# Cluster masks for the last seven pairs of heads: from TensorE products to VectorE writes ahead of the scores

## The chip, the core and the metric

One core of a Trainium2 chip runs the kernel. TensorE multiplies matrices into PSUM, VectorE and ScalarE work on PSUM and SBUF, GpSimd (POOL in the profile) on SBUF only, and DMA queues move data. The engines run side by side and wait for one another by semaphores; each takes its own instructions in program order. The metric is the time of one execution on the device in microseconds, the median of several runs.

## The reference

Attention in which a query sees only the keys of its own cluster, and behind it a feed-forward network on the result.

```python
B, H, S, D = 4, 8, 768, 64           # batch, heads, positions, head size; 16 clusters per head
q_assign = argmax(q_n @ c_n.T)       # q_n, k_n, c_n: rows scaled to length one
k_assign = argmax(k_n @ c_n.T)
mask   = q_assign[..., :, None] == k_assign[..., None, :]
scores = where(mask, q @ k.T / sqrt(D), -1e9)
attn   = softmax(scores)
x      = (attn @ v)                  # -> (3072 tokens, 512)
h = x @ w_in                         # 512 -> 2048
g = h * clip(h + 3, 0, 6) / 6
out = g @ w_out                      # 2048 -> 512
```

## The kernel before

Heads go in 16 pairs (4 pairs are a batch). A pair has 12 items: two halves of 384 queries times six chunks of 128 keys. An item is a 128 x 768 block of scores (keys x queries, both heads of the pair), in one of two buffers `ps`. Items are worked in steps of two; r is the number of the step's first item within its pair (0, 2, ... 10).

A masked score is made by two products that add up in PSUM: a product of one-hot cluster vectors in bf16 (`xm`; the keys' side is 1 outside the key's cluster and scaled by -2^60), and the product of keys and queries in f32 (`xf`). Where the clusters differ, -2^60 is added, and the exponential is zero.

```python
def route_turn(g, part):                     # turns the one-hots of pair g: xm
    ...
    po = scratch([P, NCH, P], "po", BF16)
    for i in range(NCH):
        nc.tensor.transpose(out=po[:, i], in_=one_hot[:, part * NCH + i], identity=ident_q)
    dst = xm[:, part * NCH : (part + 1) * NCH]
    nc.scalar.activation(out=dst, in_=po, func=ACT.Copy, scale=-FAR if part else 1.0)

def scores_part(n, x, first, last):
    g, hf, j = where(n)
    for t in range(2):                       # the two heads
        r = slice(t * D, (t + 1) * D)
        nc.tensor.matmul(st["ps", n][:, t, 0:HALF], lhsT=x[r, NCH + j],
                         rhs=x[r, hf * NHC : (hf + 1) * NHC], start=first, stop=last)
# scores(n): scores_part(n, xm, True, False), then scores_part(n, xf, False, True)

def exponentials(n):                         # ScalarE, ps -> ex; frees the buffer ps
    ...
def attn_v(n):                               # TensorE: pv += v * ex (two heads); behind item 5 of
    ...                                      # a half, ScalarE copies pv to num
def divide(n):                               # behind the last item of a half
    ...
    pd = scratch([P, 512], "pd")
    for t in range(2):
        nc.tensor.matmul(pd[t * D : (t + 1) * D], lhsT=ones, rhs=acc[:, t], start=True, stop=True)
    rcp = nump.tile([P, HALF], F32, name="rcp")
    nc.vector.reciprocal(out=rcp, in_=pd)
    nc.vector.tensor_tensor(out=num, in0=num, in1=rcp, op=ALU.mult)
    ...
```

`scratch` in the second half of the kernel takes its tile from a PSUM pool of one buffer (`psum_t`); `pd`, the transposes `pqk` of keys and queries, the cluster scores `pcs`, their transposes `pr` and `po` all use it. The network's products use another pool of two buffers (`psum_m`).

From pair 8 on, two kinds of steps alternate. At r = 2, 6, 10 ("fill steps") there are two scores products, two exponentials, then four or five items of the feed-forward network, with the preparation of the next pair spread among them. At r = 0, 4, 8 ("value steps") there are two scores products, two exponentials and the value products of four items, and at r = 4 and r = 8 a division.

```python
def four_by_four(n, r, steps):
    for i in steps:
        scores(i)
    if r % 4 == 2:                           # fill step: the items follow in the main loop
        for i in steps:
            exponentials(i)
        unmasked.extend(steps)
        check_all()
        ...
        return
    for i in steps[: 1 if r == 8 else 2]:
        exponentials(i)
    check_all()
    for i in unmasked:
        masks(i)                             # nothing: no pair is masked by VectorE here
        key_sums(i)                          # GpSimd: acc += ex
    unmasked.clear()
    if r == 4 or n >= total:
        ...
            later.append(divide(m))
    for i in range(st["valued"], min(n, total)):
        attn_v(i)
        if i % per_pair == NCH - 1:          # this is at r = 8
            later.append(divide(i))
    st["valued"] = min(n, total)
    for i in steps[1 if r == 8 else 2 :]:
        exponentials(i)
    for i in steps:
        masks(i)
        key_sums(i)

# main loop, pair 8 on
prep = ...      # of the next pair: r = 2: three turns (pqk); r = 6: cluster scores, route; r = 10: one-hots turned
if prep and r == (6 if fours else 4):
    prep.pop(0)()
...
for i in range(max(len(prep), want)):        # want: four or five
    if i < want:
        fill.pop(0)()
    if i < len(prep):
        prep[i]()
```

The feed-forward items of a block of 256 tokens are 8 "up" and 7 "down" items. An up item (`halved`) makes two PSUM tiles, uX and uY, from the pool of two, and VectorE adds them up:

```python
X = psum_m.tile(..., name="uX", tag="m")
part(X[:, 0], ...); part(X[:, 1], ...); part(X[:, 2], ...)         # TensorE
nc.vector.tensor_copy(out=sx[:, 1], in_=X[:, 1])
add(sx[:, 0], X[:, 0], sx[:, 1]); add(sx[:, 2], X[:, 2], sx[:, 0]) # VectorE
Y = psum_m.tile(..., name="uY", tag="m")
part(Y[:, 0], ...); ... part(Y[:, 3], ...)                         # TensorE
add(sx[:, 3], Y[:, 0], sx[:, 0]); add(g[:, 3], Y[:, 0], sx[:, 2])
add(g[:, 0:3], Y[:, 1:4], sx[:, 1:4])                              # VectorE
lift(sx, g)                                                        # ScalarE
finish()                       # clip (VectorE) and sums (GpSimd) of the up item before
```

A down item multiplies `g_sb` with the second weights into tiles X and Y of the same pool; VectorE has little to do there.

Of the kernel before, what the change touches and what calls it, by code (L numbers as in the profile page):

```python
# [8 lines left out]
F32 = mybir.dt.float32  # L9
# [8 lines left out]
C = 16  # L18
# [98 lines left out]
def fast_path(ctx, tc, ok, q, k, v, centroids, moe_w_in, moe_w_out, out):  # L117
# [48 lines left out]
    counts = const.tile([P, 2, NPAIR], F32, name="counts")  # L166
    w_low = const.tile([P, 1], F32, name="w_low")

    MASKED = NPAIR
    st = {}  # L170
    later = []
    numbers = []
# [87 lines left out]
    cen = startp.tile([P, D], F32, name="cen")  # L260
    parity = const.tile([P, 2], F32, name="parity")

    number = const.tile([P, C], BF16, name="number")

    def constants():
        make_identity(nc, ident)
        for t in range(2):
            nc.vector.tensor_reduce(
                out=parity[:, t : t + 1],
                in_=ident.rearrange("p (h t c) -> p t h c", t=2, c=C)[:, t], axis=AX.XY, op=ALU.max,  # L270
            )
        nc.gpsimd.memset(half_c, 0.5)
        nc.gpsimd.memset(low_c, 1.0 / BOUND)
        nc.gpsimd.memset(ones, 1.0)
        nc.gpsimd.memset(w_low, W_LOW)
        nc.gpsimd.memset(one_hot, 0.0)
        for c in range(C):
            nc.gpsimd.memset(number[:, c : c + 1], float(c))

        warm = psum_t.tile([P, 4, P], F32, name="warm", tag="t")  # L280
        for i in range(14):
            nc.tensor.transpose(out=warm[:, i % 4], in_=ident, identity=ident)
# [47 lines left out]
    def route(g):  # L330
        cs = st.pop(("cs", g))
        pr = scratch([P, NC2, 2, C], "pr")
        for i in range(NC2 // 4):
            nc.tensor.transpose(out=pr[:, 4 * i : 4 * i + 4], in_=cs[:, i], identity=ident)
        pr = pr.rearrange("p j t c -> p (j t) c")
        mx = rtp.tile([P, 2 * NC2], F32, name="mx")
        nc.vector.reduce_max(out=mx, in_=pr, axis=AX.X)
        oh = one_hot.rearrange("p j (t c) -> p j t c", t=2)[:, :, :, 0:C]
        pr = pr.rearrange("p (j t) c -> p j t c", t=2)
        mx = mx.rearrange("p (j t) -> p j t", t=2)  # L340
        halves = [slice(0, NCH), slice(NCH, NC2)]
        for sl, op in zip(halves, (ALU.is_ge, ALU.is_lt)):
            nc.vector.tensor_tensor(
                out=oh[:, sl], in0=pr[:, sl],
                in1=mx[:, sl].unsqueeze(3).to_broadcast([P, NCH, 2, C]), op=op,
            )


        def count():
            for a, sl in enumerate(halves):  # L350
                seen = rtp.tile([P, NCH, 2, C], BF16, name="seen")
                nc.scalar.activation(
                    out=seen, in_=oh[:, sl], func=ACT.Copy, scale=1.0 - 2 * a,
                    accum_out=counts[:, a, g : g + 1],
                )

        later.append(count)
        if g >= MASKED:
            numbers.append(lambda: clusters(g))

    def route_turn(g, part):
        if part == 0:
# [11 lines left out]
        return where(n)[0] >= MASKED  # L374

    def clusters(g):
        oh = one_hot.rearrange("p j (t c) -> p j t c", t=2)[:, :, :, 0:C]
        which = rtp.tile([P, NC2, 2, C], BF16, name="which")
        nc.vector.tensor_tensor(
            out=which, in0=oh, in1=number.unsqueeze(1).unsqueeze(1).to_broadcast([P, NC2, 2, C]), op=ALU.mult  # L380
        )
        qid = st["qid"] = rtp.tile([P, NCH, 2], BF16, name="qid")
        kid = st["kid", g] = kidp.tile([P, NCH, 2], F32, name="kid")
        nc.vector.tensor_reduce(out=kid, in_=which[:, NCH:], axis=AX.X, op=ALU.add)

        nc.vector.tensor_scalar(
            out=kid, in0=kid, scalar1=-1.0, scalar2=C * (C - 1) / 2.0, op0=ALU.mult, op1=ALU.add
        )
        qsum = rtp.tile([P, NCH, 2], F32, name="qsum")
        nc.vector.tensor_reduce(out=qsum, in_=which[:, 0:NCH], axis=AX.X, op=ALU.add)  # L390
        nc.vector.tensor_copy(out=qid, in_=qsum)

    def spread(g, part):
        if part == 0:
# [14 lines left out]

    def scores_qk(n):  # L410
        st["ps", n] = psum_s.tile([P, 2, 512], F32, name="ps")
        scores_part(n, st["xf", where(n)[0]], True, by_vector(n))

    def scores_part(n, x, first, last):
        g, hf, j = where(n)
        for t in range(2):
            r = slice(t * D, (t + 1) * D)
            nc.tensor.matmul(  # L418
                st["ps", n][:, t, 0:HALF], lhsT=x[r, NCH + j],
                rhs=x[r, hf * NHC : (hf + 1) * NHC], start=first, stop=last,  # L420
            )

    def scores(n):
        g, hf, j = where(n)
        if ("ps", n) not in st:
            if hf == j == 0 or by_vector(n):
                scores_qk(n)
            else:  # L430
                st["ps", n] = psum_s.tile([P, 2, 512], F32, name="ps")
                scores_part(n, st["xm", g], True, False)
                scores_part(n, st["xf", g], False, True)
                return
        if not by_vector(n):
            scores_part(n, st["xm", g], False, True)

    def exponentials(n):
        sc = st.pop(("ps", n))[:, :, 0:HALF]
        ex = st["ex", n] = expp.tile([P, 2, HALF], F32, name="ex")  # L440
        nc.scalar.activation(out=ex, in_=sc, func=ACT.Exp, scale=SM_SCALE)  # L441

    def masks(n):
        g, hf, j = where(n)
        if not by_vector(n):
            return
        ex = st["ex", n]
        for t in range(2):
            nc.vector.scalar_tensor_tensor(
                out=ex[:, t].rearrange("p (a b) -> p a b", b=P),  # L450
                in0=st["xm", g][:, t * NCH + hf * NHC : t * NCH + (hf + 1) * NHC],
                scalar=st["kid", g][:, j, t : t + 1], in1=ex[:, t].rearrange("p (a b) -> p a b", b=P),
                op0=ALU.is_equal, op1=ALU.mult,
            )

    def key_sums(n):
# [27 lines left out]


    def divide(n):
        g, hf, _ = where(n)
        b, kt = divmod(g, NKT)
        if kt == 0 and hf == 0:
            st["xd", b] = dram.tile([P, NKT, S], F32, name=f"xd{b}")  # L490
        acc, num = st.pop(("acc", g, hf)), st.pop(("num", g, hf))
        pd = scratch([P, 512], "pd")
        pd = pd[:, 0:HALF]
        for t in range(2):
            nc.tensor.matmul(  # L495
                pd[t * D : (t + 1) * D], lhsT=ones, rhs=acc[:, t], start=True, stop=True
            )
        rcp = nump.tile([P, HALF], F32, name="rcp")
        nc.vector.reciprocal(out=rcp, in_=pd)  # L499
        nc.vector.tensor_tensor(out=num, in0=num, in1=rcp, op=ALU.mult)  # L500

        def keep():
            nc.sync.dma_start(st["xd", b][:, kt, hf * HALF : (hf + 1) * HALF], num)
            in_range(2 * g + hf, rcp)
            if (kt, hf) == (NKT - 1, 1):
                later.append(lambda: (waiting.extend((b, m) for m in range(NHC)), load_block()))

        return keep


    def in_range(i, rcp):
# [309 lines left out]
    HOLD = 6  # L821
    st["early"] = st["free"] = True
    st["last"] = False
    fill, checks, unmasked = [], [], []
    st["done"], st["valued"] = 0, DECODED - lag_v

    def check_all():
# [8 lines left out]
# [3 lines that stand above are left out]
        if r % 4 == 2:  # L839
            for i in steps:  # L840
                exponentials(i)
            unmasked.extend(steps)
            check_all()
            for op in numbers:
                op()
            numbers.clear()
            return


        for i in steps[: 1 if r == 8 else 2]:  # L850
            exponentials(i)
        check_all()
        for i in unmasked:
            masks(i)
            key_sums(i)
        unmasked.clear()
        if r == 4 or n >= total:
            m = n - r % per_pair - 1 if n < total else total - 1
            if ("acc", *where(m)[:2]) in st and m < st["valued"]:
                later.append(divide(m))  # L860
                ready(m)
        for i in range(st["valued"], min(n, total)):
            attn_v(i)
            if i % per_pair == NCH - 1:
                later.append(divide(i))
        st["valued"] = min(n, total)
        for i in steps[1 if r == 8 else 2 :]:
            exponentials(i)
        for i in steps:
            masks(i)  # L870
            key_sums(i)

    with tc.manual_schedule():
        nc.scalar.dma_start(cen, centroids.rearrange("h c d -> (h c) d"))
# [17 lines left out]
        for n in range(0, total + lag_d + 2, 2):  # L892
# [6 lines left out]
            else:  # L899
# [8 lines left out]
                if m >= 0 and m % NCH == NCH - 1:  # L908
                    later.append(divide(m))
                    ready(m)  # L910
            if prep and r == (6 if fours else 4):
                prep.pop(0)()
            if n == DECODED:
                st["early"] = False
# [3 lines left out]
            if not fours or r % 4 == 2 or n >= total:  # L918
                want = min(items_by(n + 2) - st["done"], len(fill))
                st["done"] += want  # L920
                for i in range(max(len(prep), want)):
                    if i < want:
                        fill.pop(0)()
                    if i < len(prep):
                        prep[i]()
            if r == 6 and fours:
                load(g + 2, "q", "k")
                load(g + 1, "v")
# [384 lines left out]
```

## Time and profile before

Three runs took 1013.29 us in the median (1012.73 to 1019.36).

| Engine | busy us | share of the span |
|---|---|---|
| TensorE, products | 990.2 | 98% |
| TensorE, weight loads | 736.4 | 73% |
| VectorE | 569.3 | 56% |
| GpSimd | 433.0 | 43% |
| ScalarE | 390.3 | 38% |

The span of the profiled execution is 1014.4 us. The last two fifths of it by stretches of 50 us:

| us | TensorE | VectorE | ScalarE | GpSimd |
|---|---|---|---|---|
| 610 to 660 | 49.51 | 22.59 | 17.78 | 28.61 |
| 660 to 710 | 49.84 | 27.39 | 17.96 | 17.77 |
| 710 to 760 | 50.00 | 16.29 | 12.45 | 17.30 |
| 760 to 810 | 50.00 | 24.19 | 11.00 | 20.51 |
| 810 to 860 | 50.00 | 26.59 | 6.53 | 8.49 |

Attention ends at about 800 us; what follows is the rest of the feed-forward network. In the lines of a profile, PE is TensorE's products and PEld its weight loads, DVE is VectorE, ACT ScalarE, POOL GpSimd; "L418" is the line in the kernel; `out<-in` names the tiles; a line of a timeline has start, length, engine, line, operation, tiles, shapes and count, and in brackets the idle time before it with what ended it. Matmuls are pipelined, so lengths of neighbours overlap and their starts tell more.

### The profile page before, as it was taken

The numbers are of one execution on the slowest core, as the hardware profiler recorded it, in microseconds if no ns is written. First come the engines' busy times: TensorE is split into PE (matmuls) and PEld (weight loads), VectorE is DVE, ScalarE is ACT, GpSimd is POOL, SyncE is SP. The second block draws the span as 40 slices with busy tenths as digits, with TensorE's granted clock in tenths as the row PEclk, the third lists the DMA queues.
The fourth block names the chain that finished last, engine by engine and source line by source line (L and its number), as shares of the span: only waits on it lengthen the run. The fifth ranks groups of instructions, "written<-read, shape, count | busy, mean of one in ns | idle before, by whom it ended". The sixth has DMA issues, their size and how long they took to land.

```text
span 1014.4 us, 16737 instructions
## 1 busy us (share of the span) xinstructions
PE 990.2 (98%) x6560; PEld 736.4 (73%) x6560; DVE 569.3 (56%) x1085; ACT 390.3 (38%) x764; POOL 433.0 (43%) x363
## 2 busy tenths in 40 slices
PE   7999989999999999999999999999999999999997
PEld 4444445455778787778787777778787898999996
DVE  5899987868955245236336237237146372727270
ACT  6889866766233233233323333334223120202010
POOL 3777657666515416425506416525516130303030
PEclk9999999999999999999999999999999999999999
DMA  6355554423253052223322224123033051414120
GB/s 174 106 146 146 165 147 117 125 71 84 86 170 98 9 139 83 55 76 87 76 83 82 65 68 124 38 65 113 21 92 92 15 149 37 142 39 129 48 67 25
DMA packets 87560, 92.70 MB, mean 91 GB/s; under 512 B 53936, under 2 KB 68272, under 8 KB 87472
## 3 DMA queue, kind: packets, MB, share of 16 engines
q1 hardware_dynamic: 87328, 91.51, 31.5%
q8 instruction: 54, 0.88, 0.3%
q14 instruction: 34, 0.28, 0.1%
q10 hardware_dynamic: 144, 0.03, 0.0%
HBM read 75.79 MB, written 15.73 MB: 90 GB/s over the span
## 4 chain that ended last, share of the span: by engine, by line
PE 83%; DVE 2%; ACT 1%; issue 0%; ACTq 0%
PE Y L693 16%; PE uY L658 15%; PE X L693 12%; PE uX L658 12%; PE ps L418 11%; PE pv L474 9%; PE ph L613 3%; PE pd L495 2%; PE pqk L310 1%; PE pcs L323 1%; PE po L367 1%; ACT g_sb L523 0%; ACT xm L369 0%; DVE sx L669 0%; DVE g_sb L526 0%
## 5 line engine op out<-in xcount | busy, mean ns | idle before, releaser
L464 POOL TENSOR_TENSOR acc<-acc,ex 128x768 f32<-128x768 f32 x128 | 241.1, 1883 | 139.0 <-ACT ex L441 132.4
L648 POOL TENSOR_TENSOR g_sb<-g_sb 128x256 f32<-128x256 f32 x176 | 129.4, 757 | 318.1 <-DVE g_sb L526 296.8
L441 ACT ACTIVATE ex<-ps 128x768 f32<-128x768 f32 x192 | 148.4, 805 | 84.4 <-PE ps L418 83.8
L523 ACT ACTIVATE sx<-g_sb,half_c 128x512 f32<-128x512 f32 x88 | 63.6, 723 | 268.2 <-DVE g_sb L669 268.2
L418 PE MATMUL ps<-xf 64*128 64x384 f32 x768 | 157.1, 487 | 0.9 <-ACT ex L441 0.9
L474 PE MATMUL pv<-ex,vt 128*64 128x384 f32 x768 | 141.1, 496 | 0.0
L700 DVE TENSOR_TENSOR y<-y,Y 128x256 f32<-128x256 f32 x48 | 20.2, 421 | 169.9 <-PE Y L693 169.1
L474 PEld LDWEIGHTS pv<-ex,vt 128*64 128x64 f32 x768 | 48.7, 136 | 82.4 <-issue 73.8
L499 DVE RECIPROCAL rcp<-pd 128x384 f32<-128x384 f32 x32 | 81.8, 2555 | 40.4 <-PE pd L495 40.2
L461 POOL TENSOR_TENSOR acc<-ex 128x768 f32<-128x768 f32 x32 | 60.6, 1895 | 94.4 <-ACT ex L441 94.3
L658 PE MATMUL uX<-xb,w_in_sb 128*128 128x128 f32 x704 | 93.0, 275 | 0.0
L693 PE MATMUL X<-w_out_sb,g_sb 128*128 128x256 f32 x384 | 89.7, 381 | 0.0
L693 PE MATMUL Y<-T,g_sb 128*128 128x256 f32 x384 | 87.3, 380 | 0.0
L693 PE MATMUL Y<-w_out_sb,g_sb 128*128 128x256 f32 x384 | 87.2, 380 | 0.0
L658 PEld LDWEIGHTS uX<-xb,w_in_sb 128*128 128x128 f32 x704 | 85.7, 192 | 0.0
L418 PEld LDWEIGHTS ps<-xf 64*128 64x128 f32 x768 | 67.8, 188 | 21.2 <-issue 17.6
L693 PEld LDWEIGHTS X<-w_out_sb,g_sb 128*128 128x128 f32 x384 | 71.2, 190 | 12.9 <-issue 3.5
L693 PEld LDWEIGHTS Y<-T,g_sb 128*128 128x128 f32 x384 | 72.3, 190 | 11.2 <-issue 1.7
L693 PEld LDWEIGHTS Y<-w_out_sb,g_sb 128*128 128x128 f32 x384 | 72.2, 190 | 11.1 <-issue 1.1
L418 PE MATMUL ps<-xm 64*128 64x384 bf16 x384 | 61.0, 327 | 7.0 <-ACT ex L441 3.8
L526 DVE SCALAR_TENSOR_TENSOR g_sb<-sx,g_sb 128x512 f32<-128x512 f32 x88 | 67.1, 768 | 0.9 <-ACT sx L523 0.9
L669 DVE TENSOR_TENSOR g_sb<-uY,sx 128x128 f32<-128x128 f32 (+1 forms) x176 | 65.7, 415 | 0.0
(110 smaller groups left out, 1389.2 us busy)
## 6 DMA issues: line engine op xcount, KB each, us to landing
tx<-td SPq DMA_DIRECT2D x86, 384.0 KB, 3.2
raw<-in_moe_w_in_dram SPq DMA_DIRECT2D x16, 512.0 KB, 3.8
raw<-in_moe_w_out_dram SPq DMA_DIRECT2D x16, 512.0 KB, 3.7
qk<-in_q_dram SPq DMA_DIRECT2D x32, 192.0 KB, 4.5
qk<-in_k_dram SPq DMA_DIRECT2D x32, 192.0 KB, 4.9
vt<-in_v_dram SPq DMA_DIRECT2D x32, 192.0 KB, 3.8
xd<-num SPq DMA_DIRECT2D x32, 192.0 KB, 2.7
xb<-xd SPq DMA_DIRECT2D x12, 512.0 KB, 4.1
```

Of the source, the lines that this page charges most:

```text
L418: nc.tensor.matmul(st["ps", n][:, t, 0:HALF], lhsT=x[r, NCH + j], rhs=x[r, hf * NHC : (hf + 1) * NHC], start=first, stop=last,)
L441: nc.scalar.activation(out=ex, in_=sc, func=ACT.Exp, scale=SM_SCALE)
L461: nc.gpsimd.tensor_tensor(out=acc, in0=st["ex", n - 1], in1=ex, op=ALU.add)
L464: nc.gpsimd.tensor_tensor(out=acc, in0=acc, in1=ex, op=ALU.add)
L474: nc.tensor.matmul(pv[t * D : (t + 1) * D], lhsT=vt[:, t, j], rhs=ex[:, t], start=(j == 0), stop=(j == NCH - 1),)
L499: nc.vector.reciprocal(out=rcp, in_=pd)
L523: nc.scalar.activation(out=r, in_=h, func=ACT.Relu, bias=half_c, scale=1.0 / 6.0)
L526: nc.vector.scalar_tensor_tensor(out=g, in0=r, scalar=1.0, in1=h, op0=ALU.min, op1=ALU.mult)
L648: eng.tensor_tensor(out=out_, in0=in0, in1=in1, op=op)
L658: nc.tensor.matmul(dst, lhsT=w[:, kt], rhs=x(kt), start=(kt == 0), stop=(kt == HK - 1))
L669: nc.vector.tensor_tensor(out=out_, in0=in0, in1=in1, op=ALU.add)
L693: nc.tensor.matmul(bank[:, half * HC : (half + 1) * HC], lhsT=g_sb[:, kind, i], rhs=w[:, i], start=(first and i == 0), stop=(last and i == ...
```

## The change

For pairs 9 to 15 (seven of sixteen) the one-hot product leaves TensorE. VectorE writes the mask itself into the bank of the scores, before the scores product, which then adds onto it: for each item and head it compares the queries' cluster numbers (`xm`, now spread over all partitions) with the key's number, writes -2^60 where they differ, and zero where they agree. The mask of item n + 2 can be written once the exponential of item n has read the bank.

- In a fill step the masks of the next two items (four instructions, `singles`) stand behind the first items of the feed-forward network, two behind each; at r = 6 and r = 10 from the second item on. None is behind the last.
- In a value step they stand right behind the exponentials.
- The division is cut in two: its products stay where they were, the reciprocal and the multiplication (`inverse`) follow at the end of the step, behind the masks.
- The numbers of the clusters come from a weighted sum of the one-hots on VectorE (`clusters`), and `spread` brings them onto all partitions with 12 small bf16 products in three groups, in place of the 12 transposes in two groups of `route_turn`. The first group stands in front of the fill at r = 10.
- The sums over the keys on GpSimd (`key_sums`) of a fill step no longer wait for the next step.

It is meant to relieve TensorE, using VectorE's idle time. The core of the diff:

```diff
-    MASKED = NPAIR
+    MASKED = NPAIR // 2 + 1
...
+        def weigh():
+            for h in range(2):
+                nc.vector.tensor_tensor(
+                    out=which[:, h], in0=oh[:, h],
+                    in1=number[:, h].unsqueeze(1).unsqueeze(1).to_broadcast([P, NCH, 2, C]), op=ALU.mult,
+                )
+        def collect():
+            nc.vector.tensor_reduce(out=kid, in_=which, axis=AX.X, op=ALU.add)
+        def narrow():
+            nc.vector.tensor_copy(out=qid, in_=kid[:, 0])
+        return [weigh, collect, narrow]
...
     def scores(n):
+        if by_vector(n):
+            scores_part(n, st["xf", g], False, True, True)
+            return
...
-    def masks(n):
+    def masks(n, heads=(0, 1)):
...
+        if ("ps", n) not in st:
+            st["ps", n] = psum_s.tile([P, 2, 512], F32, name="ps")
+        for t in heads:
+            nc.vector.tensor_scalar(
+                out=st["ps", n][:, t, 0:HALF].rearrange("p (a b) -> p a b", b=P),
                 in0=st["xm", g][:, t * NCH + hf * NHC : t * NCH + (hf + 1) * NHC],
+                scalar1=st["kid", g][:, 1, j, t : t + 1], scalar2=-FAR,
+                op0=ALU.not_equal, op1=ALU.mult,
             )
...
@@ four_by_four, fill step
-            unmasked.extend(steps)
+            for i in steps:
+                key_sums(i)
             check_all()
+            for t in range(2):
+                singles.extend(lambda i=i, t=t: masks(i, [t]) for i in (n + 2, n + 3))
             return
@@ four_by_four, value step
         for i in steps[: 1 if r == 8 else 2]:
             exponentials(i)
         check_all()
+        for i in steps[: 1 if r == 8 else 2]:
+            masks(i + 2)
...
-                later.append(divide(i))
+                inverse = sum_up(i)
         st["valued"] = min(n, total)
         for i in steps[1 if r == 8 else 2 :]:
             exponentials(i)
+        for i in steps[1 if r == 8 else 2 :]:
+            masks(i + 2)
         for i in steps:
-            masks(i)
             key_sums(i)
+        if inverse:
+            later.append(inverse())
@@ main loop
-            if prep and r == (6 if fours else 4):
+            if prep and (r in (6, 10) if fours else r == 4):
                 prep.pop(0)()
...
+                    for _ in range({6: 2 * (i > 0), 10: 2 * (i > 0)}.get(r, 2)):
+                        if singles:
+                            singles.pop(0)()
+                if fours:
+                    for op in singles + numbers:
+                        op()
+                    singles.clear(), numbers.clear()
```

## Prediction

> **What bounds the kernel now.** I read the page first (busy times, the chain that ended last), then the chain piece by piece, the timeline of all engines in some steps of the second half, and the groups by shape.
>
> ```profile
> PE 990.2 (98%) x6560; PEld 736.4 (73%) x6560; DVE 569.3 (56%) x1085; ACT 390.3 (38%) x764; POOL 433.0 (43%) x363
> ...
> PE 83%; DVE 2%; ACT 1%; issue 0%; ACTq 0%
> ```
>
> TensorE is never idle and is the chain. What leaves it shortens the kernel, unless something else makes it wait. The work to leave is the mask product. In TensorE's timeline one value step begins like this (start, length, operation):
>
> ```profile
> 741.51 0.34 PE L418 MATMUL ps<-xm 64*128 64x384 bf16 x2
> 741.68 0.81 PE L418 MATMUL ps<-xf 64*128 64x384 f32 x4
> 742.33 0.33 PE L418 MATMUL ps<-xm 64*128 64x384 bf16 x2
> 742.49 0.81 PE L418 MATMUL ps<-xf 64*128 64x384 f32 x4
> 743.23 0.87 PE L495 MATMUL pd<-acc,ones 128*64 128x384 f32 x4
> ```
>
> Lengths overlap, so I read the starts: a pair of mask matmuls holds TensorE from 741.51 to 741.68 and from 742.33 to 742.49, 0.165 us an item; the f32 part holds it 0.65 us. The group's mean of 327 ns would be twice too much.
>
> Now the step with the division inside a pair (r = 8) and the fill step behind it, pair 14:
>
> ```profile
> 699.71 0.81 PE L495 MATMUL pd<-acc,ones 128*64 128x384 f32 x4
> 699.87 0.19 ACT L352 ACTIVATION_READ_ACCUMULATOR seen<-one_hot 128x1 f32 x1
> 699.96 0.46 ACT L480 COPY num<-pv 128x384 f32<-128x384 f32 x1
> 700.32 0.81 ACT L441 ACTIVATE ex<-ps 128x768 f32<-128x768 f32 x1
> ...
> 700.57 2.56 DVE L499 RECIPROCAL rcp<-pd 128x384 f32<-128x384 f32 x1 [1.89 <-PE pd L495]
> ...
> 703.64 0.71 PE L658 MATMUL uX<-xs,tx 128*128 128x128 f32 x4
> ```
>
> The reciprocal starts as soon as pd is there and ends at 703.13, 0.5 us before TensorE reaches the fill (703.64). pd lies in the pool of one buffer that every transpose and scratch product of the preparation uses too.
>
> Last, what a burst on VectorE between two up items costs already: the routing of the next pair sits there.
>
> ```profile
> 684.29 0.68 DVE L526 SCALAR_TENSOR_TENSOR g_sb<-sx,g_sb 128x512 f32<-128x512 f32 x1
> ...
> 684.89 0.55 DVE L337 TENSOR_REDUCE mx<-pr 128x24 f32<-128x384 f32 x1
> ...
> 685.48 0.62 DVE L343 TENSOR_TENSOR one_hot<-pr,mx 128x192 bf16<-128x192 f32 x2
> ...
> 686.02 0.28 DVE L676 COPY sx<-uX 128x128 f32<-128x128 f32 x1
> ...
> 686.33 0.62 DVE L669 TENSOR_TENSOR sx<-uX,sx 128x128 f32<-128x128 f32 x2
> ...
> 687.00 0.71 PE L658 MATMUL uX<-xs,tx 128*128 128x128 f32 x4 [0.16 <-DVE sx L669]
> ```
>
> The burst (684.89 to 686.02, 1.13 us) pushes the three sx operations back, and the next uX product, whose bank they free, starts at 687.00 in place of 686.68 (uX at 683.55 plus 1.34 and 1.79 for uX and uY in the chain).
>
> **What the Trainium skill says.** "VectorE: DVE Perf Modes", section "Why PSUM operands drop a tier": an operand in PSUM shuts out the modes with two ports, leaving for f32 one element a cycle. So the bf16 input makes the mask no faster. The trace agrees for what it has: the 128x128 f32 copy out of PSUM takes 291 ns, the 128x256 f32 addition 421 ns, 128x512 elements 689 ns, all about 155 ns plus 1.04 ns an element. "SBUF — State Buffer", section "Who interferes with whom": a VectorE instruction with at most one SBUF input outside those modes doesn't contend with GpSimd; one with two does. The trace agrees on the second half: the clip with two SBUF inputs takes 0.68 us, and 1.06 us where GpSimd works (697.62). No run yet shows a mask into PSUM. "PSUM — Partial Sum Buffer", section "The four PSUM rules": VectorE writes leave the bits alone that decide between adding and overwriting, so a product without a start flag adds onto the mask where an earlier product set them; this costs nothing in time.
>
> **The change, part by part.**
>
> (1) Removed: mask matmuls of 7 pairs x 12 = 84 items. 84 x 0.165 = 13.9 us off TensorE. All on the path.
>
> (2) Transposed one-hots (12 bf16 matmuls a pair, twice 0.34 us in the chain) become 12 bf16 matmuls in three groups, some 3 x 0.23 = 0.69 us. Equal: 0. ScalarE: two copies of 0.81 us become three of 0.59 us. 0.
>
> (3) Added on VectorE: 168 masks of 128x384. By the row above 155 + 384 x 1.04 = 555 ns; the small operations with a per-partition scalar run some 30 ns longer (251 against 226 ns for 64 elements), so 0.58 us, two 1.16 us, all 168 about 97 us. From 510 to 810 us VectorE is more than half idle on most stretches (16 to 27 us busy in each 50 us), so they fit on average. What counts is where they stand in its order.
>
> (4) Masks behind up items, 42 pairs of masks. Each item period: uX 1.34 + uY 1.79 = 3.13 us on TensorE; VectorE 0.94 + 0.95 + 0.68 = 2.6 us. VectorE must finish the sx operations of item k+1 before uX of item k+2. From uX of item k: uY ends at 3.13; additions, clip to 4.88; masks to 6.04; sx of k+1 to 6.98; uX of k+2 was due at 6.26. So 0.76 us of waiting, less the preparation between the items (0.44 us of transposes behind each of the first three at r = 2, hence none there; 0.23 us behind one at r = 10), and 0.6 for a second burst in a row. (The same sum with 1.13 us and the 0.33 us of pr gives 0.40 for the routing; the trace has 0.32.) It only counts when k+1 is an up item and the fill goes on. Counting the fill order (53 items per 48, 8 up then 7 down): r = 10 of pair 8: 0.53 + 0.6; r = 10 of pair 9: 0.53; r = 6 of pairs 12, 13, 14, 15: 0.6, 1.2, 1.2, 0.76. Sum 5.4 us, and some 0.2 us for each of nine restarts (the chain has 1.60 in place of 1.34 for uX behind such a wait): 7 us. Behind down items masks are free: VectorE waits there anyway.
>
> (5) The reciprocal goes behind the masks of its step. At r = 8 the second exponential ends at 701.13 (700.32 + 0.81), two masks run to 702.3, the reciprocal to 704.9 in place of 703.13. TensorE comes four mask products earlier, 703.64 - 0.66 = 702.98. Now the first spread product has been moved to the very start of this fill (the diff adds r = 10 to the pop), and its scratch bank is pd's. It waits until 704.9: 1.9 us, 1.5 where the second exponential isn't held up by ScalarE; say 1.7. Pairs 9 to 14: 6 x 1.7 = 10.2 us.
>
> (6) The same at r = 4, then r = 6, where the cluster scores stand in front: before, 1.69 us lay between the reciprocal's end (677.59) and the cluster scores (679.28). Where the fill before ends with an up item, its lift holds the exponentials: they end at 674.9 and 675.6, four masks run to 677.3, the reciprocal starts 2.24 us later than now (675.03). 2.24 + 0.66 - 1.69 = 1.2 us of waiting in pairs 10 to 14; 0.4 in pair 9 (a down item before): 6.4 us.
>
> (7) Small: the second scores product at r = 10 waits 0.15 us for its mask in some pairs (1 us), the first sx operations of the last fill come behind the later reciprocal (0.7 us). 1.7 us. Sums on GpSimd move one step earlier, off the path.
>
> Sum: -13.9 + 7 + 10.2 + 6.4 + 1.7 = +11.4 us.
>
> **The rivals.** First: the waits are hidden and only the 13.9 us count: 999.4 us. For it: VectorE half idle, masks placed with care behind the first items and during the value products (2.7 us, long enough for four masks). Against it: the two places where scratch and reciprocal meet, with margins of 0.5 and 1.69 us that the trace shows. Second: masks are shorter than I think. At 0.45 us, (4) is about 3, (5) 9.6, (6) 3: +3.5 us, 1017. Third: VectorE becomes the bound in up fills, every masked pair costing 0.76 us: 20 of the 42 stand between two up items, 15 us in place of 7: 1033. Against it: the preparation leaves room at r = 2. Fourth: a new wait on GpSimd, as the clip meets its sums more often: 12 fills x 0.4 us at most, +5 us.
>
> **Range and chances.** The sum gives 1024.7; the shorter mask 1017. I weigh the first about twice: 1022 us. The range from 1010 (half of (5) and (6) isn't there) to 1032 (third and fourth rival in part). A gain of 2% would need 20 us, more than all that is removed: 0.01. A loss of over 2% needs 1033.6: 0.08.
>
> **What would show it.** In the changed profile: the xm group of ps at 216 matmuls (384 - 168); masks of about 0.58 us, 168 of them; TensorE waiting on the reciprocal in front of the spread product (six times, 1.5 to 1.9 us) and of the cluster scores (six times, 0.4 to 1.2); uX waiting on sx nine times more. VectorE busy near 570 + 97, and some 9 more for the cluster numbers (7 x about 1.3 us). I am wrong if TensorE's waits on the reciprocal don't appear, or if the masks take under 0.4 us; then the time falls below 1010.

## Result and profile after

The changed kernel takes 1025.27 us in the median (1024.8 to 1026.16) against 1013.63 us before: ratio 1.0108, 95% interval 1.0074 to 1.0143. It is slower by 11.6 us; predicted were 8.7 in the figure and 11.4 in the sum.

The page of the changed kernel: busy times, chain that ended last.

```profile
PE 984.4 (96%) x6392; PEld 730.6 (71%) x6392; DVE 666.9 (65%) x1281; ACT 389.5 (38%) x771; POOL 432.8 (42%) x379
...
PE 78%; DVE 10%; ACT 7%; issue 3%; DMA 2%; SPq 1%; ACTq 0%; DVEq 0%
```

TensorE has 168 products less, but the chain has changed hands: VectorE and ScalarE, 3% of it before, hold 17%. The groups by shape show the work itself as expected: 168 masks of 615 ns, 216 mask matmuls left.

```profile
L460 DVE TENSOR_SCALAR ps<-xm,kid 128x384 f32<-128x384 bf16 x168 | 97.9, 615 | 30.9 <-ACT ex L451 28.0 <-ACT xm L409 1.1
...
L424 PE MATMUL ps<-xm 64*128 64x384 bf16 x216 | 34.4, 327 | 7.1 <-ACT ex L451 3.9 <-ACT xm L370 2.8
```

What TensorE waited for (who, for whom; us, times, longest):

```profile
PE pb L405 <- DVE rcp L515: 8.7, 6, 1.4
PE pcs L324 <- DVE rcp L515: 6.1, 6, 1.1
...
PE uX L676 <- DVE sx L687: 1.0, 5, 0.4
```

Neither of the first two stood in the profile before. Six first spread products (pb) and six cluster-score products (pcs) now wait for the reciprocal. The timeline of pair 14 from the division at r = 8 on (the step shown before):

```profile
709.04 0.81 ACT L451 ACTIVATE ex<-ps 128x768 f32<-128x768 f32 x1
...
709.89 1.27 DVE L460 TENSOR_SCALAR ps<-xm,kid 128x384 f32<-128x384 bf16 x2 [0.55 <-ACT ex L451]
...
710.63 1.59 PE L424 MATMUL ps<-xf 64*128 64x384 f32 x8
711.07 2.55 DVE L515 RECIPROCAL rcp<-pd 128x384 f32<-128x384 f32 x1
...
713.67 0.38 PE L405 MATMUL pb<-ident_q,qid 128*128 128x128 bf16 x4 [1.45 <-DVE rcp L515]
```

Exponential, two masks, reciprocal, one behind the other; the spread product starts 0.05 us behind the reciprocal's end (713.62), after TensorE has stood still for 1.45 us.

To see where each microsecond sits I took from TensorE's timelines the start of the first scores product of every two-item step; the distance to the next is the step's length. Most steps agree between profiles to 0.02 us, so 42 steps (r = 10 of pair 8 to r = 8 of pair 15) can be compared one by one. The table sums their differences from the kernel before without the mask product of these pairs (first experiment).

```
us, against "no mask product"   r=0,4,8    r=2     r=6    r=10     all   median time
before                             5.03   1.62    0.74    1.35    8.74       1013.6
no mask product (e1)               0      0       0       0       0          1005.1
changed                           -0.03   1.25    7.09   12.56   20.87       1025.3
  bank freed early (e2)           -0.04   1.26    3.30    8.03   12.55       1017.9
  no masks in fill steps (e3)      0.46   1.23    4.97    9.87   16.53       1023.7
  no masks in value steps (e4)     0.01  -0.02    0.56    0.82    1.37       1007.5
  no masks at all (e5)             0.02  -0.01   -1.53   -0.01   -1.53       1004.1
  bank and ScalarE queue (e6)      0.00   1.16    0.56    1.34    3.06       1008.7
  spread behind first item (e7)    3.25   0.62    7.27   10.55   21.69       1027.5
  reciprocal first (e8)           -0.02   1.24    7.41   28.96   37.59       1047.8
  ScalarE queue only (e9)         -0.03   1.19    7.35   10.34   18.85       1024.0
before, early key sums (e10)       5.07   1.61    0.11    1.36    8.15       1013.6
```

The change takes 8.7 us out and puts 20.9 us in, nearly all of it at the heads of the fills at r = 6 and r = 10. (2.2 us of the 12.56 lie in one step of this profile, r = 10 of pair 12, in which a cast on VectorE stood still behind GpSimd and TensorE's clock fell; see the end. The r = 6 steps of pairs 12 and 13 hold a longer wait of their own in e1; see e10.)

### The profile page after: what moved, and what is told of

Its sections match the earlier page's. It is cut to its first block, busy times and chain, and to the rows that moved or that the text cites. A ratio compares the mean times of both kernels' runs of the same rounds, so it can differ in the third digit from the quotient of the medians.

```text
span 1024.4 us, 16650 instructions
## 1 busy us (share of the span) xinstructions
PE 984.4 (96%) x6392; PEld 730.6 (71%) x6392; DVE 666.9 (65%) x1281; ACT 389.5 (38%) x771; POOL 432.8 (42%) x379
## 4 chain that ended last, share of the span: by engine, by line
PE 78%; DVE 10%; ACT 7%; issue 3%; DMA 2%; SPq 1%; ACTq 0%; DVEq 0%
PE Y L711 16%; PE uY L676 14%; PE X L711 12%; PE uX L676 11%; PE ps L424 9%; PE pv L485 8%; DVE rcp L515 3%; PE ph L631 3%; ACT ex L451 3%; DVE ps L460 2%; PE pqk L311 1%; PE pd L509 1%; PE pcs L324 1%; ACT wsize L221 1%; DVE sx L687 1%
## 5 line engine op out<-in xcount | busy, mean ns | idle before, releaser
L460 DVE TENSOR_SCALAR ps<-xm,kid 128x384 f32<-128x384 bf16 x168 | 97.9, 615 | 30.9 <-ACT ex L451 28.0
L544 DVE SCALAR_TENSOR_TENSOR g_sb<-sx,g_sb 128x512 f32<-128x512 f32 x88 | 64.2, 734 | 1.3 <-ACT sx L541 1.2
```

Of the source, the lines that this page charges most:

```text
L460: nc.vector.tensor_scalar(out=st["ps", n][:, t, 0:HALF].rearrange("p (a b) -> p a b", b=P), in0=st["xm", g][:, t * NCH + hf * NHC : t * NC ...
L544: nc.vector.scalar_tensor_tensor(out=g, in0=r, scalar=1.0, in1=h, op0=ALU.min, op1=ALU.mult)
```

## The experiments

The ratios are against the kernel before in the same session, 1013.2 to 1013.9 us.

**e1, no mask product, in the kernel before** (the masks of pairs 9 to 15 are left out):

```diff
     def scores(n):
         g, hf, j = where(n)
+        if g > NPAIR // 2:
+            st["ps", n] = psum_s.tile([P, 2, 512], F32, name="ps")
+            scores_part(n, st["xf", g], True, True)
+            return
```

> The kernel before, without the mask product of pairs 9 to 15 (their masks are left out, all else as before): the gross gain of term (1) by itself. Prediction's 0.165 us an item: 13.9 us less, 999.7 us. By the profile after, where a step of two f32 scores products takes 1.49 us in the chain against 1.72 with the masks: 42 steps x 0.23 = 9.7 us less, 1003.9 us. If the mask product is hidden in part behind other things: 1008 us or more.

1005.07 us, ratio 0.9912 (0.9893 to 0.9932): 8.4 us less; by the steps 8.7. The most that the change could bring is under two thirds of the 13.9 us of term (1). TensorE's timeline of the changed kernel shows why:

```profile
750.93 1.56 PE L424 MATMUL ps<-xf 64*128 64x384 f32 x8
752.42 0.54 PE L509 MATMUL pd<-acc,ones 128*64 128x384 f32 x2
```

Two items of f32 scores hold TensorE 1.49 us, 0.745 each, where they took 0.65 each behind a mask product. So 0.23 us a step goes and not 0.33.

**e2, the bank freed early, in the changed kernel.** ScalarE copies pd to SBUF, and VectorE takes the reciprocal from there at the same place in its order.

```diff
+        got = []
+        def free():
+            got.append(nump.tile([P, HALF], F32, name="rcp"))
+            nc.scalar.copy(out=got[0], in_=pd)
         def inverse():
-            rcp = nump.tile([P, HALF], F32, name="rcp")
-            nc.vector.reciprocal(out=rcp, in_=pd)
+            rcp = got[0] if got else nump.tile([P, HALF], F32, name="rcp")
+            nc.vector.reciprocal(out=rcp, in_=rcp if got else pd)
...
         for i in steps[1 if r == 8 else 2 :]:
             exponentials(i)
+        if inverse:
+            inverse.free()
```

> The changed kernel, but ScalarE copies pd from PSUM to SBUF behind the step's last exponential, and VectorE takes the reciprocal from the copy. The order on VectorE stays. If the loss of terms (5) and (6) is the bank that the late reciprocal holds: the waits of the first spread product and of the cluster scores on the reciprocal go (8.7 and 6.1 us in the profile after), about 1011 us. Rival, the late reciprocal itself: the next VectorE work comes as late as before, TensorE waits for it a product further on (uX on sx), 1018 to 1025 us.

1017.93 us, ratio 1.0055 (1.0037 to 1.0073): 7.3 us less than the changed kernel, half of what the theory said. TensorE's waits on the reciprocal are gone, and others stand in their place. TensorE's waits:

```profile
PE pb L405 <- ACT xm L409: 5.6, 7, 1.0
...
PE pr L335 <- ACT cs L329: 1.6, 2, 1.0
```

And the timeline of this kernel at r = 10 of pair 14:

```profile
704.85 1.18 DVE L522 TENSOR_TENSOR num<-num,rcp 128x384 f32<-128x384 f32 x1
...
706.06 0.52 ACT L537 ACTIVATE rcp<-rcp 128x384 f32<-128x384 f32 x1 [1.70 <-DVE num L522]
...
706.71 0.61 ACT L538 ACTIVATE rcp<-rcp,low_c 128x384 f32<-128x384 f32 x1
...
707.33 0.56 ACT L409 CAST xm<-pb 128x512 bf16<-128x512 f32 x1
...
707.94 0.38 PE L405 MATMUL pb<-ident_q,qid 128*128 128x128 bf16 x4 [1.00 <-ACT xm L409]
```

ScalarE stands idle for 1.70 us in front of the division's range check (`in_range`, two activations on rcp), which needs VectorE's multiplication; the copy of the first spread product waits behind it in ScalarE's order, and the second spread product, which needs the same bank, waits for that copy. The rival was right in that the wait moved, wrong in where: into ScalarE's queue, not to the uX products.

**e3, e4, e5, masks left out of the fill steps, of the value steps, or of both, in the changed kernel.** The masks of half the items, or of all, of pairs 9 to 15 are left out; their scores products start their banks afresh.

```diff
+    def left_out(n):                       # fill steps: n % 4 < 2; value steps: n % 4 >= 2; all: True
+        return n < total and by_vector(n) and n % 4 < 2
...
     def scores(n):
+        if left_out(n):
+            st["ps", n] = psum_s.tile([P, 2, 512], F32, name="ps")
+            scores_part(n, st["xf", g], True, True)
+            return
...
     def masks(n, heads=(0, 1)):
-        if n >= total or not by_vector(n):
+        if n >= total or not by_vector(n) or left_out(n):
             return
```

> The changed kernel without the 84 masks that stand behind feed-forward items in fill steps (left out; the scores product of these items starts its bank afresh). Term (4): 7 us less, 1018 us, and the uX products' waits on sx fall back to the three that the kernel before has. Rival, VectorE as the bound of every up fill: 15 us less, 1010 us. If bursts behind up items cost nothing: 1025 us.

> The changed kernel without the 84 masks that stand behind the exponentials of value steps (left out). Terms (5) and (6), and the small ones of (7): the reciprocal comes earlier by the masks before it, 15 us less, 1010 us; the first spread product may still wait some 0.3 us a pair, as the reciprocal still follows the step's last exponential. If only the masks' length and not their order counts, e3 and e4 give the same, about 7 us less each.

> The changed kernel with all 168 masks left out; everything else of the change stays (numbers of the clusters, spread products, their place in front of the fill, reciprocal behind the step). If the masks' time on VectorE is all that the loss comes from: as the kernel before without the mask product, 1005 us, 1 us more at most for the spread. If the moved spread product and the later reciprocal cost something without masks too: 1008 us or more.

Without the fill steps' masks 1023.68 us, ratio 1.0092 (1.0071 to 1.0114): 1.6 us less, which lies within the scatter of the two, where term (4) said 7; by the steps 4.3, or 2.1 without r = 10 of pair 12. Without the value steps' masks 1007.46 us, ratio 0.9938 (0.9918 to 0.9957): 17.8 us less. Without any 1004.05 us, ratio 0.9919 (0.9897 to 0.9941). The loss hangs on the masks of the value steps, which stand in front of the reciprocal. The fill steps' masks alone cost 1007.46 - 1004.05 = 3.4 us (the intervals of the two overlap); by the steps 1.37 + 1.53 = 2.9. Cluster numbers, spread products and the deferred reciprocal cost nothing by themselves.

**e6, bank and ScalarE's queue, in the changed kernel.** The range check is also moved behind the second feed-forward item (and with it the store of `num`, which stands in front of it).

```diff
@@ on top of the bank freed early: four_by_four, fill step
-            check_all()
+            if n >= total:
+                check_all()
@@ main loop
                     if i < len(prep):
                         prep[i]()
+                    if fours and r % 4 == 2 and i == 1:
+                        check_all()
```

> The kernel of the run with the bank freed early (1017.9 us), and the check of the division's range, which holds ScalarE until VectorE has multiplied, moved from in front of the fill to behind its second item. If what was left there was the same late reciprocal, now met in ScalarE's queue (spread product waiting for the copy of the one before, 3.7 us in the profile, transposes waiting for the cluster scores' copy, 1.6 us, and hidden ones): 1009 to 1012 us, under the kernel before. If it is VectorE's lateness itself (sx behind the multiplication): 1016 to 1018 us.

1008.71 us, ratio 0.9962 (0.9951 to 0.9974). It writes all 168 masks on VectorE and is faster than both kernels. The r = 10 of pair 14 in its timeline:

```profile
692.81 2.54 DVE L521 RECIPROCAL rcp<-rcp 128x384 f32<-128x384 f32 x1
...
693.39 1.51 ACT L451 ACTIVATE ex<-ps 128x768 f32<-128x768 f32 x2 [1.43 <-issue]
...
693.90 0.40 PE L405 MATMUL pb<-ident_q,qid 128*128 128x128 bf16 x4
...
694.79 0.59 ACT L409 CAST xm<-pb 128x512 bf16<-128x512 f32 x1
695.39 1.18 DVE L522 TENSOR_TENSOR num<-num,rcp 128x384 f32<-128x384 f32 x1
```

The spread product runs while the reciprocal is still under way, its copy has begun before the multiplication, and TensorE has no wait in brackets. The reciprocal is as late as in the changed kernel: at r = 10 of pair 14 it ends 2.98 us behind the start of the step's first scores product, there 2.99. Lateness alone costs little: r = 10 is 0.5 us longer than without the value steps' masks (1.34 against 0.82). What costs is what queues behind it.

**e9, ScalarE's queue only, with pd still in its bank** (the last diff alone).

> The changed kernel with the range check moved behind the second feed-forward item (as in the run at 1008.7 us), but VectorE still reads pd from its bank. If the bank's wait and the wait in ScalarE's queue lie one behind the other and add up: the bank's 8.7 and 6.1 us stay, the other half goes, about 1016 us. If they lie side by side, so that only both together bring it: 1022 to 1025 us. If ScalarE's queue was all: 1009 us.

1024.03 us, ratio 1.0096 (1.0078 to 1.0114): 1.2 us less than the changed kernel, within the scatter of the two. TensorE's waits on the reciprocal are all still there:

```profile
PE pb L405 <- DVE rcp L515: 8.7, 6, 1.4
PE pcs L324 <- DVE rcp L515: 6.3, 6, 1.1
```

So the two waits don't add. While the bank holds TensorE back, ScalarE has time to work off its queue; take the bank's wait away, and the queue's shows. The bank alone brings 6.1 of 18.7 us (20.87 less the 2.2 of pair 12), the queue alone next to nothing, both 15.6.

**e7, the spread product back behind the first item, in the changed kernel** (undoing one line of the change; the masks at r = 10 move one item back too):

```diff
-            if prep and (r in (6, 10) if fours else r == 4):
+            if prep and r == (6 if fours else 4):
...
-                    for _ in range({6: 2 * (i > 0), 10: 2 * (i > 0)}.get(r, 2)):
+                    for _ in range({6: 2 * (i > 0), 10: 2 * (i > 1)}.get(r, 2)):
```

> The changed kernel, but the first spread product at r = 10 is back behind the first feed-forward item, and the masks there behind the third and fourth. If term (5) is the meeting of spread product and reciprocal: 8.7 us and what stands behind it go, 1014 to 1017 us. If the late reciprocal strikes elsewhere: 1020 us or more.

1027.48 us, ratio 1.014 (1.0115 to 1.0165): not better, and my expectation was wrong. The spread product no longer waits for the reciprocal, but TensorE waits at the next value step instead. Its waits:

```profile
PE ps L424 <- DVE ps L460: 7.8, 5, 2.4
PE pcs L324 <- DVE rcp L515: 6.1, 6, 1.1
```

The end of r = 10 of pair 13:

```profile
654.75 0.59 ACT L409 CAST xm<-pb 128x512 bf16<-128x512 f32 x1 [3.10 <-PE pb L405]
...
658.26 0.87 DVE L718 TENSOR_TENSOR y<-y,Y 128x256 f32<-128x256 f32 x2 [5.59 <-PE Y L711]
659.05 1.13 DVE L460 TENSOR_SCALAR ps<-xm,kid 128x384 f32<-128x384 bf16 x2
659.72 1.56 PE L424 MATMUL ps<-xf 64*128 64x384 f32 x8 [1.50 <-DVE ps L460]
```

The last copy of the spread product is done at 655.34. The masks start at 659.05, because they now stand behind the last item, whose addition waits for Y on VectorE. So it is the new place of the masks that costs here. The run moved both, and doesn't show whether the spread product had to stand in front of the fill.

**e8, the reciprocal in front of the second item's masks at r = 8, in the changed kernel:**

```diff
+        if inverse and r == 8:
+            later.append(inverse())
+            inverse = None
         for i in steps[1 if r == 8 else 2 :]:
             masks(i + 2)
```

> The changed kernel, but at r = 8 the reciprocal stands in front of the masks of the step's second item. The bank is free 1.2 us earlier, and these masks are 2.6 us later: the second scores product of r = 10 waits for them, about 1.5 us in each of seven pairs in place of the spread product's wait. 1023 to 1027 us if order only moves the wait; 1018 us or less if the deferral of the reciprocal is itself the fault.

1047.83 us, ratio 1.0348 (1.0327 to 1.0368). I had expected a wait of 1.5 us to take the other's place; TensorE waited 19.3 us in seven times, up to 4.6:

```profile
726.34 1.27 DVE L460 TENSOR_SCALAR ps<-xm,kid 128x384 f32<-128x384 bf16 x2
...
727.75 1.10 PE L424 MATMUL ps<-xf 64*128 64x384 f32 x4 [2.24 <-DVE ps L460]
```

The multiplication goes with the reciprocal, and after such waits TensorE runs on a lower clock (end of this text). Deferring the reciprocal was right.

**e10, early key sums, in the kernel before** (one part of the change alone):

```diff
             for i in steps:
                 exponentials(i)
-            unmasked.extend(steps)
+            for i in steps:
+                key_sums(i)
             check_all()
```

> The kernel before with one part of the change alone: GpSimd's sums over the keys of a fill step no longer wait for the next step. In the run without any masks the two r = 6 steps of pairs 12 and 13 are 0.5 and 0.6 us shorter than in the kernel before beyond the mask products: VectorE's clip there doesn't meet GpSimd. Expected 1 to 2 us less in all, 1011.5 to 1012.5 us; if that came from the missing masks, the same as before within 0.5 us.

1013.60 us, ratio 0.9992 (0.9982 to 1.0001): no difference that the times can tell. The steps show 0.6 us at r = 6, under the 1 to 2 us I expected: the 0.5 and 0.6 us of the expectation still held 0.23 us of mask product each, and without it they are 0.27 and 0.33. The 1.53 us that the run without any masks gains at r = 6 against e1 lie in the same two steps, in the wait of uX for sx. In the kernel before it is 0.44 and 0.49 us, without the mask product (e1) 0.90 and 0.95, here 0.17 twice, and without any masks, where the key sums come early too, 0.16 twice: 0.74 and 0.79 less than in e1. TensorE, relieved of the mask product, ran further into a wait that the early key sums take away.

## Why the prediction held

The time lies within the range, 3.3 us above the figure and 0.6 us above the sum. Its parts were less exact than the sum.

- **(1) mis-sized.** "0.165 us an item", 13.9 us in all; measured 0.115 an item in most steps, which for 84 items is 9.7 us; 8.7 us by the steps and 8.4 by the times, as two steps wait 0.46 us longer for VectorE (see e10). I read how long the mask product held TensorE while the f32 product followed it. Without it the f32 product takes 0.095 us longer. What in TensorE makes it so was not tried.
- **(2) right.** The run without masks has the same r = 10 steps as the kernel before without the mask product (-0.01 us): spread for turned one-hots is an even trade.
- **(3) nearly right.** 615 ns a mask against 580; 97.9 us on VectorE against 97. The page of the Trainium skill that I took for it, "VectorE: DVE Perf Modes", section "Why PSUM operands drop a tier", limits f32 with an operand in PSUM to the slowest mode; that a bf16 input gains nothing where the output is f32 in PSUM was my inference from it, and the 615 ns agree. By the 1.04 ns an element of other shapes, 384 elements are 399 ns; the rest is by this estimate 216 ns where I took 180. (A slip in the second rival: masks 0.13 us shorter, two at each of six places, bring term (5) to 8.6 us and not 9.6.)
- **(4) mis-sized by half.** 7 us predicted, 2.9 by the steps and 3.4 by the times. It shows in the six places that the term names, at 0.2 to 0.7 us each, and TensorE's list has five waits of uX for sx in place of three, where nine more were foretold. "0.76 us of waiting" (6.98 - 6.26 is 0.72) adds up durations, but on VectorE the next instruction starts before the one in front has ended in the profile. An up item of r = 6 in pair 14 of the changed kernel:

```profile
695.01 0.29 DVE L687 TENSOR_TENSOR sx<-uY,sx 128x128 f32<-128x128 f32 x1
...
695.22 0.75 DVE L687 TENSOR_TENSOR g_sb<-uY,sx 128x128 f32<-128x128 f32 x2
...
695.88 0.68 DVE L544 SCALAR_TENSOR_TENSOR g_sb<-sx,g_sb 128x512 f32<-128x512 f32 x1
...
696.48 1.14 DVE L460 TENSOR_SCALAR ps<-xm,kid 128x384 f32<-128x384 bf16 x2
...
697.52 0.28 DVE L694 COPY sx<-uX 128x128 f32<-128x128 f32 x1
...
697.84 0.62 DVE L687 TENSOR_TENSOR sx<-uX,sx 128x128 f32<-128x128 f32 x2
...
698.51 0.71 PE L676 MATMUL uX<-xs,tx 128*128 128x128 f32 x4
698.52 0.29 DVE L687 TENSOR_TENSOR sx<-uY,sx 128x128 f32<-128x128 f32 x1
```

From start to start (695.01 to 698.52) VectorE's period is 3.51 us, not 2.6 + 1.16 = 3.76. And uX comes on time here (the chain's uX and uY before it, from 695.10: 1.60 + 1.80 gives 698.50), as the routing had already set TensorE back; I charged the wait again. The third rival, VectorE as the bound of all up fills, fell with it. At r = 2 I had expected no wait behind masked items, and the run with these masks alone has none (-0.02 us).
- **(5) right, with half of its mechanism.** 1.7 us a pair predicted, six waits of 1.45 measured (8.7 us against 10.2). The bank that the reciprocal holds is what ends last, and with the bank freed it is gone. But "it waits until 704.9" left out that ScalarE's range check waits for the same late VectorE work in front of the copies: freeing the bank brought 7.3 us of the time, and only with the queue mended did the rest come. From my steps the kernel with the bank freed would have been 16.6 us faster, 9 us more than it is.
- **(6) right.** 1.2 us five times and 0.4 once predicted; the trace has 1.1 five times and about 0.4 once, and r = 6 loses 7.09 - 0.56 = 6.5 us to the value steps' masks, against 6.4.
- **(7) right in size, wrong in place.** Second scores products that wait for their masks cost 1.25 us, but at r = 2, behind the masks of r = 0, and at r = 10 only in one pair. (At r = 2 of pair 10 the second product starts 0.99 us behind the first, in e1 0.75; the list of waits counts 0.07 us of it.)

By the steps the parts add up like this: -9.7 (mask product) - 0.6 (key sums, in no term) + 2.9 (4) + 9.5 (5) + 6.5 (6) + 1.3 (7) + 2.2 (r = 10 of pair 12, in no term) = +12.1 us. Term (1) was 4 us too hopeful and term (4) 4 us too gloomy; that these errors cancelled was luck. The rival "all waits are hidden" is refuted by the twelve waits. The fourth rival, GpSimd, shows in one step only: at r = 8 of pair 12 the cast of the cluster numbers stood still behind it, the reciprocal ended 0.54 us later than in e9, and TensorE waited 0.31 us for a mask at r = 10.

## What to carry to other kernels

When an in-order engine gets new work in front of an old instruction, list everything that instruction releases, its PSUM bank as well as the other engines' queues, and ask what stands there next; a wait that is taken away shows the one that lay beside it. A product's worth to its engine is the change in start-to-start distance without it, so leave it out once and measure before building its replacement. And compare kernels step by step from the starts of one recurring instruction: steps that agree to 0.02 us show a loss of 0.3 us that a total doesn't.

## What the runs showed of the hardware

- TensorE's granted clock was halved for 3.41 us behind a stretch of 3.41 us in which TensorE stood idle for about half the time. In the changed kernel's profile this is r = 10 of pair 12, where the waits of 0.31 and 1.45 us fall into one such stretch (TensorE busy for 1.66 us; the number after the five engines is the clock):

```profile
567.50:570.91 3.41, 1.66 (x13) 1.08 (x11) 3.27 (x3) 1.70 (x3) 2.54 (x3) 1.00 0.00 0
570.91:574.32 3.41, 3.41 (x10) 2.69 (x9) 0.00 (x0) 1.72 (x5) 1.56 (x1) 0.50 0.16 58
574.32:577.73 3.41, 3.41 (x20) 2.96 (x19) 1.47 (x3) 0.86 (x2) 0.00 (x0) 1.00 0.00 0
```

The 128x256 products there take 634 ns in place of 379, and the step 2.2 us more than in two other kernels with the wait of 1.45 us alone (23.46 against 21.23 and 21.24 us): 0.54 us by which the spread product comes later, and about 1.7 us, half of 3.41, of clock. Five other waits of 1.45 us left the clock alone. With the reciprocal first (e8), the clock was halved six times while the changed pairs ran (for 3.41 us, once for 6.83), each time behind 3.41 us with TensorE busy for 0.00 to 1.17 us, and the six starts (366.55, 506.49, 578.17, 656.68, 728.36 and 796.62) lie whole multiples of 3.413 us apart. One stretch there with 1.66 us busy left the clock alone, so the limit lies near half, and is not shown closer. The page of the Trainium skill "TensorE: Matmul & The Clock Gate", section "The HAM clock gate", has a clock that halves after an idle window of about 3.4 us; the halving and the length agree, but here about half of a window idle was enough.
- Two masks into the two banks of one scores tile start 0.66 us apart (682.34 and 683.00), two into different tiles 0.53 us (683.00 and 683.53). The cause was not tried.
- A cast of 128x12 elements on VectorE, 0.17 us elsewhere, took 1.80 us (563.54 to 565.34) where it began 0.04 us behind the start of an addition on GpSimd (563.50 to 565.31); in e9, where it began 0.02 us ahead of it, it took 0.17. The two 128x192 products before it took 1.46 together in place of 0.42. So small operations between SBUF tiles can stand still for a whole GpSimd instruction. This agrees with the Trainium skill, "SBUF — State Buffer", section "Who interferes with whom", which says of VectorE's two-port modes, open to casts, that whoever starts first has the ports shared with GpSimd for the whole instruction.
